# Retention and a mixture of experts on one core: the first two batches in another token layout, with 64x64 score tiles and states summed afresh

## The chip, the cores and the metric

One core of a Trainium2 chip. The metric is the device time of one launch in microseconds (us), all runs below being in the undisturbed state ("fast") by the granted clock and by agreement with the other runs of the same kernel. A profile is one execution taken by the hardware profiler; its span is about 1.7 us shorter than the launch's time.

Two words for the tensor engine (TensorE, PE): I call it **full rate** where a 512-column matmul follows the last after 0.216 us and **half rate** where it takes 0.43 us. The prediction says "fast state" and "slow state" for the same thing. Read the rate from the spacing of the matmuls: the clock column of the views reads 1.00 for the start, though 128 columns take 0.106 us through most of it, as against 0.057 at full rate.

## The reference

```python
# q, k, v: [8 batches, 8 heads, 576 tokens, 64], float32
scores = q @ k.transpose(0, 1, 3, 2) / sqrt(64)
Dmat   = where(i >= j, gamma[h] ** (i - j), 0)           # decay, one gamma for each head
x      = ((scores * Dmat) @ v)                           # retention
x      = x.transpose(0, 2, 1, 3).reshape(4608, 512)      # tokens x (heads * 64)
p      = domain_probs / domain_probs.sum(-1)
out    = sum over 4 experts of  p[:, e] * (relu(x @ w1[e]) @ w2[e])   # 512 -> 1024 -> 512
```

## The kernel before

Expert work is done in nine tiles of 512 tokens. Each tile has 48 groups, 12 for each expert (8 of the first matrix, then 4 of the second), 256 matmuls of 128x512 in all. While tile `nt` runs, the retention of batch `nt + 1` is put between its groups by a plan (`at(group, function)`). Batch 0 must be done before the first tile. Decay is split into factors on k (`gk`) and on the result (`gq`), so a chunk of 128 tokens needs its own masked scores and the state, the sum of `k^T v` over all earlier chunks. Two heads share a "pair". An eviction copies a result of TensorE out of PSUM, the memory that it writes to; a mask is VectorE's copy of the scores with those above the diagonal set to zero.

```python
    def load(b, gate=None):                      # 24 transfers of 128 KB in 256 B packets
        t = {n: raw.tile([128, NCH, H, D], FP32, tag=n, name=f"raw_{n}") for n, _ in SRC}
        for p in range(NP):
            for n, src in SRC:
                for h in (2 * p, 2 * p + 1):
                    i = nc.sync.dma_start(out=t[n][:, :, h, :],
                                          in_=src[b, h, 0:SM, :].rearrange("(c p) d -> p c d", p=C))
        # ... cut: gate: the first transfer waits for another DMA

        def kv(self, n, pairs):                  # the chain: add chunk n to the state in PSUM, copy it out
            # ... cut: matmuls into self.kvp
            for j in (0, 64):
                nc.scalar.activation(sbd[n][j:j + 64, a:z, j:j + 64],
                                     self.kvp[j:j + 64, a:z, j:j + 64], Copy)

    for p in allp:                               # batch 0, one pair after the other
        casts0(p)
        if p > 0:
            a0.O([p - 1])                        # outputs of the last pair
        a0.T(p)                                  # transposes of q and k
        a0.kv(0, [p])
        a0.S([p])                                # scores, masks
        for n in range(1, NCH):
            a0.kv(n, [p])
    # ... cut: weights of experts 1 to 3
    load(1, a0.w20)                              # batch 1, released when w2 of expert 0 has landed

        if nt == 0:                              # the plan of tile 0
            # ... cut: the remainder (tokens 512 to 575) of batch 0
            for p, g in zip(allp, (22, 31, 40, 44)):
                at(g - 4, *[lambda p=p, n=n: state["a1"].cast(n, p, nc.gpsimd) for n in "kqv"])
                at(g, lambda p=p: state["a1"].T(p), lambda p=p: state["a1"].kv(0, [p]))
                at(g + 1, lambda p=p: state["a1"].kv(1, [p]), lambda p=p: state["a1"].S([p]))
                at(g + 2, lambda p=p: state["a1"].kv(2, [p]))
                at(g + 3, lambda p=p: state["a1"].kv(3, [p]), lambda p=p: state["a1"].O([p]))
            at(46, lambda: state["a1"].cast_rem(nc.gpsimd))
            at(47, lambda: state["a1"].Trem(), lambda: state["a1"].Srem(), lambda: state["a1"].Orem())
            at(47, lambda: load(2), lambda: load_rem(2))
```

Later batches are transposed by DMA instead of TensorE and run inside full tiles.

## Time and profile before

| | before |
|---|---|
| time, median | 591.28 us (587.73 to 591.89, 3 runs) |
| span of the profiled run | 590.0 us |
| TensorE busy | 94% of the span |
| start, until the first expert matmul | 28.3 us |
| tile 0, tile 1, tile 2 | 75.5, 70.1, 60.3 us |

"Busy" counts time with an instruction in flight; for pipelined matmuls that is not peak use. To see where a tile loses time, compare it with a tile in the steady state: tile 2 and those after it are full. The prediction below shows the view of these stretches, the waits and the two holes.

### The profile page before, as it was taken

The numbers are of one execution on the slowest core, as the hardware profiler recorded it, in microseconds if no ns is written. First come the engines' busy times: TensorE is split into PE (matmuls) and PEld (weight loads), VectorE is DVE, ScalarE is ACT, GpSimd is POOL, SyncE is SP. The second block draws the span as 40 slices with busy tenths as digits, with TensorE's granted clock in tenths as the row PEclk, the third lists the DMA queues.
The fourth block names the chain that finished last, engine by engine and source line by source line (L and its number), as shares of the span: only waits on it lengthen the run. The fifth ranks groups of instructions, "written<-read, shape, count | busy, mean of one in ns | idle before, by whom it ended". The sixth has DMA issues, their size and how long they took to land.

```text
span 590.0 us, 8114 instructions
## 1 busy us (share of the span) xinstructions
PE 554.6 (94%) x3223; PEld 262.9 (45%) x3284; DVE 162.7 (28%) x268; ACT 232.3 (39%) x446; POOL 89.5 (15%) x131
## 2 busy tenths in 40 slices
PE   3698798779999999999999999999999999999997
PEld 2344354334444444444444444444444444444443
DVE  5512136004420442034303430343124311220222
ACT  5443343443236323632354335433453344335332
POOL 3510320342400411031203130223000000000000
PEclk9999799979999999999999999999999999999999
DMA  8999922948225901490149104820400010010001
GB/s 200 187 202 201 214 55 75 211 103 193 54 80 90 223 1 59 96 224 17 53 100 214 28 37 111 188 59 19 124 11 1 4 69 1 0 49 23 1 0 71
DMA packets 155157, 53.82 MB, mean 91 GB/s; under 512 B 144332, under 2 KB 148428, under 8 KB 155120
## 3 DMA queue, kind: packets, MB, share of 16 engines
q1 hardware_dynamic: 148848, 44.92, 31.9%
q0 software_dynamic: 6272, 8.39, 8.1%
q8 instruction: 25, 0.41, 0.3%
q14 instruction: 12, 0.10, 0.1%
HBM read 45.16 MB, written 9.44 MB: 93 GB/s over the span
## 4 chain that ended last, share of the span: by engine, by line
PE 84%; DMA 8%; SPq 5%; issue 1%; POOL 1%; ACT 0%; DVE 0%; POOLq 0%
PE po L305 40%; PE ph L298 38%; SPq L80 5%; DMA raw_v<-in_v_dram 4%; DMA wt_276<-in_moe_w_dram 3%; PE o L265 1%; PE kvp L195 1%; PE o L270 1%; POOL vm L182 1%; DMA raw_q<-in_q_dram 0%; POOL qm L182 0%; DVE acc L312 0%; PE orem L281 0%; PE pt L208 0%; PE orem L285 0%
## 5 line engine op out<-in xcount | busy, mean ns | idle before, releaser
L300 ACT ACTIVATE hT<-ph 128x512 bf16<-128x512 f32 x288 | 171.9, 597 | 263.8 <-PE ph L298 260.2
L305 PEld LDWEIGHTS <-hT 128*128 128x128 bf16 x1152 | 112.2, 99 | 139.2 <-issue 9.0
L312 DVE SCALAR_TENSOR_TENSOR acc<-po,probs,acc 128x512 f32<-128x512 f32 x108 | 81.1, 751 | 324.3 <-PE po L305 282.8
L298 PE MATMUL ph<-xT,wt_383 128*128 128x512 bf16 x281 | 66.3, 383 | 0.4
L305 PE MATMUL po<-wt_276,hT 128*128 128x512 bf16 x285 | 66.0, 386 | 0.3 <-issue 0.2
L305 PE MATMUL po<-wt_381,hT 128*128 128x512 bf16 x279 | 65.2, 386 | 1.1 <-issue 0.9
L298 PE MATMUL ph<-xT,wt_387 128*128 128x512 bf16 x279 | 65.4, 380 | 0.4
L298 PE MATMUL ph<-xT,wt_379 128*128 128x512 bf16 x279 | 65.3, 379 | 0.5
L298 PE MATMUL ph<-xT,wt_274 128*128 128x512 bf16 x280 | 64.0, 383 | 0.6 <-issue 0.2
L305 PE MATMUL po<-wt_385,hT 128*128 128x512 bf16 x279 | 63.6, 379 | 0.5
L305 PE MATMUL po<-wt_389,hT 128*128 128x512 bf16 x281 | 63.5, 379 | 0.4
L177 POOL TENSOR_TENSOR km<-raw_k,gk 128x512 bf16<-128x512 f32 x28 | 29.3, 1047 | 203.9 <-DMA raw_k<-in_k_dram 110.0
L298 PEld LDWEIGHTS <-wt_274 128*128 128x128 bf16 x288 | 28.4, 99 | 34.2 <-issue 1.6
L298 PEld LDWEIGHTS <-wt_383 128*128 128x128 bf16 x288 | 27.4, 98 | 31.8 <-issue 1.0
L298 PEld LDWEIGHTS <-wt_379 128*128 128x128 bf16 x288 | 27.3, 98 | 29.3
L298 PEld LDWEIGHTS <-wt_387 128*128 128x128 bf16 x288 | 26.9, 98 | 29.5
L310 ACT ACTIVATE acc<-po,probs 128x512 f32<-128x512 f32 x36 | 24.7, 687 | 38.1 <-PE po L305 37.1
L195 PE MATMUL kvp<-vm,km 128*128 128x128 bf16 x128 | 18.1, 230 | 16.0 <-POOL vm L182 11.4
L182 POOL CAST vm<-raw_v 128x512 bf16<-128x512 f32 x32 | 18.6, 613 | 80.2 <-PE o L265 60.8
L274 DVE TENSOR_TENSOR xT<-o,gq 128x512 bf16<-128x512 f32 x32 | 21.0, 688 | 19.4 <-PE o L270 18.8
L195 PEld LDWEIGHTS <-km 128*128 128x128 bf16 x128 | 10.7, 101 | 18.2 <-issue 11.5
L182 POOL CAST qm<-raw_q 128x512 bf16<-128x512 f32 x28 | 16.1, 612 | 10.4 <-DMA raw_q<-in_q_dram 10.4
(231 smaller groups left out, 249.4 us busy)
## 6 DMA issues: line engine op xcount, KB each, us to landing
out_dram<-acc SPq DMA_DIRECT2D x36, 256.0 KB, 2.0
raw_k<-in_k_dram SPq DMA_DIRECT2D x64, 128.0 KB, 2.9
raw_q<-in_q_dram SPq DMA_DIRECT2D x64, 128.0 KB, 2.8
raw_v<-in_v_dram SPq DMA_DIRECT2D x64, 128.0 KB, 2.8
wt_274<-in_moe_w_dram POOLq DMA_DIRECT2D x1, 1024.0 KB, 9.7
raw_kr<-in_k_dram SPq DMA_DIRECT2D x8, 128.0 KB, 3.5
wt_276<-in_moe_w_dram POOLq DMA_DIRECT2D x1, 1024.0 KB, 15.9
raw_qr<-in_q_dram SPq DMA_DIRECT2D x8, 128.0 KB, 3.2
```

Source lines behind the costliest of these rows:

```text
L80: i = nc.sync.dma_start(out=t[n][:, :, h, :], in_=src[b, h, 0:SM, :].rearrange("(c p) d -> p c d", p=C))
L177: self.gate[n, p] = eng.tensor_tensor(o, i, gk[:, 0:NCH, h].unsqueeze(3).to_broadcast([128, NCH, 2, D]), op=MULT)
L182: self.gate[n, p] = eng.tensor_copy(o, i)
L195: nc.tensor.matmul(self.kvp[:, p, :], lhsT=flat(self.m["k"][:, n, h, :]), rhs=flat(self.m["v"][:, n, h, :]), start=(n == 0 and i == 0), st ...
L265: nc.tensor.matmul(o[64 * j:64 * j + 64, c * C:(c + 1) * C], lhsT=self.m["v"][:, c, 2 * p + j, :], rhs=self.sT[p][:, j, c, :], start=(c == ...
L270: nc.tensor.matmul(o[:, c * C:(c + 1) * C], lhsT=sbd[c - 1][:, p, :], rhs=self.qkT[:, 0, p, c * C:(c + 1) * C], start=False, stop=(c == NC ...
L274: nc.vector.tensor_tensor(xT[:, p, b * S:b * S + SM], o, gq[:, p, 0:SM], op=MULT)
L298: nc.tensor.matmul(ph, lhsT=w1_sb[e][:, dc, fc * 128:(fc + 1) * 128], rhs=xT[:, dc, n0:n0 + NT], start=(dc == 0), stop=(dc == NDC - 1))
L300: nc.scalar.activation(hT[:, fc, :], ph, Relu)
L305: nc.tensor.matmul(po, lhsT=hT[:, fc, ns * 128:(ns + 1) * 128], rhs=w2_sb[e][:, fc, :], start=(fc == 0), stop=(fc == NFC - 1))
L310: nc.scalar.activation(acc[ns], po, Copy, scale=pe)
L312: nc.vector.scalar_tensor_tensor(acc[ns], po, pe, acc[ns], op0=MULT, op1=ADD)
```

## The change

The intent: load batches 0 and 1 with two neighbouring tokens on one partition, which makes packets of 512 B, in units of four heads by 256 tokens (`hf` is the half, `u` the four heads); tile the scores 64x64, so that four small matmuls run at once (no score less is computed: 16 matmuls of 64x64x128 for a unit, where a pair had 8 of 64x128x128, and the masks keep their size); sum each state from scratch, so that no state waits for the eviction of the one before; let the first three groups of tile 0 start on 256 tokens (`lead`). Batch 2 is loaded earlier, into half buffers. Not shown: k of batch 0 is cast by GpSimd instead of VectorE, w1 of expert 0 comes in two transfers, and later batches are loaded and cast by chunk. Cut to its core:

```diff
+                    if b < 2:
+                        h = slice(4 * u, 4 * u + 4)
+                        i = nc.sync.dma_start(
+                            out=pairs_of(t[n, hf])[:, h],
+                            in_=src[b, h, 256 * hf:256 * hf + 256, :].rearrange("h (p j) d -> p h (j d)", j=2))
+                    else:            # by chunk, 256 B packets as before
...
+        def kv(self, hf, u):
+            for s in range(2):
+                rows = [(slice(0, 128), x) for x in range(2 * hf)]
+                rows += [(slice(0, 64 + 64 * s), 2 * hf + j) for j in range(2)]
+                ...                  # 8 matmuls in the first half, 16 in the second
...
-    for p in allp:
-        casts0(p)
-        if p > 0:
-            a0.O([p - 1])
-        a0.T(p)
-        a0.kv(0, [p])
-        a0.S([p])
-        for n in range(1, NCH):
-            a0.kv(n, [p])
+    for x, (hf, u) in enumerate(UNITS):
+        ...                          # casts; two exponentials for gq in units 0 and 1
+        a0.T(hf, u, nc.scalar)
+        a0.kv(hf, u)
+        a0.S(hf, u)
+        a0.O(hf, u)
...
-            for p, g in zip(allp, (22, 31, 40, 44)):
+            for x, g in zip(UNITS, (17, 24, 32, 39)):
+                ...                  # casts at g-3, T at g, kv at g+1, S at g+2, O at g+5
-            at(47, lambda: load(2), lambda: load_rem(2))
+            at(37, lambda: load(2), lambda: load_rem(2))
+            ...                      # remainder of batch 1: groups 42, 43, 45, 46 instead of 46, 47
-        for g, _ in enumerate(moe(nt)):
+        for g, _ in enumerate(moe(nt, lead=3 if nt == 0 else 0)):
```

## The prediction

> **What bounds the kernel now.** I read the page first (TensorE is busy 94% of the span, the chain that ended last is 84% TensorE), then cut the span at the tile boundaries that the timeline shows: the first expert matmul starts at 28.3 us, tile 0 (512 tokens) ends at 103.8, tile 1 at 173.9, tile 2 at 234.2. The windows view of these four stretches (start:end, length, busy us and count of each engine, granted clock, DMA share, GB/s):
>
> ```profile
> 0.00:28.30 28.30, 14.02 (x125) 8.58 (x127) 15.09 (x41) 14.03 (x42) 12.09 (x24) 1.00 1.00 193
> 28.30:103.80 75.50, 68.88 (x430) 32.78 (x437) 23.91 (x41) 28.05 (x68) 12.36 (x17) 0.95 0.79 151
> 103.80:173.90 70.10, 62.48 (x366) 29.26 (x374) 17.22 (x27) 24.51 (x44) 21.61 (x30) 0.95 0.53 124
> 173.90:234.20 60.30, 59.93 (x363) 28.49 (x368) 17.55 (x27) 24.41 (x44) 10.86 (x15) 1.00 0.43 97
> ```
>
> Tile 2 is the steady state: 60.3 us, TensorE full. 256 expert matmuls at 0.216 us (eight take 1.73 us in the chain) are 55.3 us; the other 5 us are the attention of the next batch. The tiles after it repeat, the last ones without attention. So everything outside the first 174 us is at the matmul bound and the change, which touches batches 0 and 1 (and how later batches are loaded and cast, beside full tiles), can only move the first three rows: 28.3 us of start, a tile of 75.5 and a tile of 70.1.
>
> What they lose is in TensorE's waits (line, releaser: total us, times, longest):
>
> ```profile
> PE kvp L195 <- POOL vm L182: 11.4, 5, 6.2
> PE pt L208 <- ACT qm L180: 7.1, 4, 6.5
> PE kvp L195 <- ACT sbd_162 L200: 2.3, 5, 0.5
> ```
>
> and the timeline shows the two large holes, in tile 0 and in tile 1, and the slow matmuls after each:
>
> ```profile
> 61.27 0.61 POOL L182 CAST vm<-raw_v 128x512 bf16<-128x512 f32 x1 [8.59 <-DMA raw_v<-in_v_dram]
> 61.94 0.26 PE L195 MATMUL kvp<-vm,km 128*128 128x128 bf16 x1 [4.40 <-POOL vm L182]
> 62.85 2.76 PE L305 MATMUL po<-wt_381,hT 128*128 128x512 bf16 x6 [0.22 <-issue]
> ...
> 120.54 0.26 PE L195 MATMUL kvp<-vm,km 128*128 128x128 bf16 x1 [6.15 <-POOL vm L182]
> ```
>
> First hole: batch 1's v is late by DMA, TensorE waits 4.4 us, then 12 expert matmuls run at 0.43 us instead of 0.216 (2.5 us) and some attention slowly too: about 7.4 us. Second hole: the load of batch 2 is issued only at 101.8 us, after tile 0's output stores, its casts end at 120 us, and TensorE sits for over 6 us and restarts slowly. Tile 1 is 70.1 - 60.3 = 9.8 us too long. The start is a dependency chain, not a load: pair 1 of batch 0 begins at 6.50, pair 2 at 11.94, pairs 3 and 4 at 17.38 and 22.83, a period of 5.44 us, while a pair's 786 KB are issued in 3.3 us. One period:
>
> ```profile
> 6.50 0.61 PE L208 MATMUL pt<-ident,qm 128*128 128x128 bf16 x4 [6.50 <-ACT qm L180]
> 7.57 0.69 DVE L209 COPY qkT<-pt 128x1024 bf16<-128x1024 bf16 x1 [2.56 <-PE pt L208]
> ...
> 9.03 0.69 DVE L237 TENSOR_TENSOR sT<-s_197,tri 128x512 bf16<-128x512 f32 x1 [0.77 <-PE s_198 L230]
> ...
> 9.64 0.68 DVE L237 TENSOR_TENSOR sT<-s_198,tri 128x512 bf16<-128x512 f32 x1
> ...
> 10.48 0.27 PE L195 MATMUL kvp<-vm,km 128*128 128x128 bf16 x1 [0.53 <-ACT sbd_162 L200]
> ...
> 10.67 0.64 PE L265 MATMUL o<-sT,vm 128*64 128x128 bf16 x8
> ```
>
> The masks end at 10.32; the serial chain of states (matmul, ScalarE eviction, matmul) ends at 10.5. The chain that the change removes therefore lies almost wholly beside the masks: without it the outputs could start only some 0.3 us earlier.
>
> **The Trainium skill.** (1) "TensorE: Matmul & The Clock Gate", Part 1: the array runs at 1.2 GHz until about 3.4 us of sustained activity and falls back after idle of that order. The trace agrees: 0.43 us per 512 columns after the holes, 0.216 otherwise; the whole start runs slow (128 columns every 0.106 us at 6.5 to 27 us, 0.057 later). (2) "DMA: Bandwidth & Descriptors", Queues, rings and completion order: an engine takes turns between queues by packet. The trace agrees: between the release of batch 1's load at 30.8 and 61.3 us five weight matrices landed (3 x 512 + 2 x 1024 rows = 3584 packets) and some 3072 packets of 256 B of batch 1, nearly one to one. (3) Same page, Specifications: line rate wants at least 512 B per transfer. The trace has 256 B packets at about 235 GB/s alone; no run yet shows 512 B. (4) "TensorEngine Tiling (Array Packing)", Key Properties: a change of tiling mode drains the array. The trace shows it between 64-row scores and 128-row states as about 0.14 us extra when slow, about 0.1 when fast.
>
> **Part by part.**
>
> Loads of batches 0 and 1. Two tokens per partition make 512 B packets, 12 transfers of 256 KB instead of 24. Taking turns by packet, batch 1 gets twice the bytes per weight packet: one w1 (512 packets) lets 262 KB through, one w2 524 KB, so a w1 and a w2 together carry one unit's 786 KB. I estimate batch 0 landed at 13 us, w1 of expert 0 at 19.5, its w2 at 25 (before: 30.7), which releases batch 1. From the weights' spacing before (about 5.8 us a w1, 6.6 a w2, some 10% longer now), units 0 to 3 of batch 1 land at about 40, 53, 67 and 70 us. They are wanted at groups 17, 24, 32 and 39, by my sum about 51, 63, 72 and 85 us. The first hole closes: 7.4 us gained.
>
> Load of batch 2. It is placed at group 37 instead of 47, ahead of the output stores, and its buffers are halves that come free with the casts. It can run from about 72 to 87 us. Tile 1 then finds its data and should take the steady 60.3: 9.8 us gained. This is the largest and safest term.
>
> More TensorE work in tile 0. From the timeline one pair of batch 1 in the fast state displaces 0.51 (8 transposes and a state) + 0.49 + 0.06 + 0.68 = 1.74 us, four pairs 7.0. A unit after: 8 transposes 0.45; 8 or 16 state matmuls at 0.057 (each state summed from scratch) with 2 or 4 changes between 64 and 128 rows, 0.65 or 1.3; 16 scores of 64x64 (twice as many, four at a time; weight loads of 64 columns take 0.022 each) 0.65; 16 outputs and 2 to 4 state products 0.8. Sum 2.5 or 3.25, four units 11.5: 4.5 us lost. The remainder of batch 1 was a serial 2.6 us at group 47 (101.2 to 103.8); spread over groups 43 to 46 it is about 0.8: 1.8 gained. Tile 0: 75.5 - 7.4 + 4.5 - 1.8 = 70.8.
>
> The start. Scheduled unit by unit without interleaving: transposes, states, scores, outputs. In the slow state: transposes 0.85; states 1.15 or 2.3 (16 x 0.106 and four drains); scores 0.7 and 0.3 to the end; two masks 1.3 as above; outputs 0.7, drain 0.2, state products 0.2 or 0.4. Periods about 5.7 and 7.1 us, four units 25.6. First transpose: the query cast no longer stands behind four exponentials (3.1 us on ScalarE), so about 4.7 us in place of 6.5, allowing for two of them before the eviction. Experts start at 4.7 + 25.6 = 30.3, 2.0 us later than now. Should TensorE go fast, as it is denser now, transposes, states and outputs halve, periods fall to some 4.9 and 5.5 and the start ends at 25.6, 2.7 us earlier. The lead of three half-width groups only hides the last eviction, under 1 us.
>
> Sum. Slow start: -2.0 + (75.5 - 70.8 = 4.7) + 9.8 = 12.5 us less. Fast start: 2.7 + 4.7 + 9.8 = 17.2 less. I weigh them 60 to 40: 14.4 us off 591.3, so 576.9; I say 576.5.
>
> **Rivals.** (a) The start is the load, not the chain: then 512 B packets and more of them per turn would bring the experts forward by 5 us or more, total near 570. For: TensorE's longest single wait, 6.5 us, is for the first data. Against: data is issued every 3.3 us but used every 5.44. (b) The hole in tile 0 moves rather than closes: unit 2 is wanted at 72 and lands at 67 plus 2.3 us of casts (1.05 + 0.61 + 0.61), a margin of 3 us that a faster start eats. If it is missed, 2 to 4 us of wait and a slow restart: total 581 to 583. (c) 64x64 scores run no better than two at a time and the weight loads bind, 0.05 us each slow: another 3 us in start and tile 0, 580. (d) Later tiles slow because casts go by chunk: against it, GpSimd is busy 11 of 60 us there and TensorE has no waits.
>
> **Range and chances.** The two safe terms, 9.8 and 7.4, less 2.7 of surer extra work, leave 14.5; the start moves this by -3 to +6, rivals b and c by another -4. That gives 569 to 583. A 2% gain needs 579.4, which the slow start (578.8) only just meets; I put 0.75 on faster, 0.24 on same, 0.01 on slower.
>
> **What would show it.** Right: no wait for v over 1 us after the start; tile 1 at 60 to 61 us; batch 2's load issued before 80 us; tile 0 at 69 to 72; expert matmuls from 26 to 31 us; masks (0.68 each) still between scores and outputs in each unit. Wrong: experts beginning before 25 us (the chain was load or the clock); a hole in tile 0 at a unit's transposes or states; tile 1 longer than 62 us.

## The result and the profile after

The changed kernel takes **576.12 us** (574.53 to 577.0, 4 runs), against 591.59 us of the kernel before in the same comparison (4 runs, the three above among them). The ratio is 0.9747 with a 95% interval from 0.9698 to 0.9796. Ratios here are the mean time of one kernel's fast runs over that of the other's of the same rounds, so not quite the ratio of the medians quoted. The span of the profiled run is 572.8 us.

The windows view of the changed kernel, cut as before at the first expert matmul and the tile boundaries (columns as in the prediction: start:end, length, then PE, PEld, DVE, ACT and POOL busy, clock, DMA share, GB/s):

```profile
0.00:27.10 27.10, 16.92 (x220) 11.89 (x221) 11.40 (x36) 12.64 (x26) 19.35 (x35) 1.00 1.09 214
27.10:96.20 69.10, 67.94 (x542) 34.25 (x549) 25.74 (x54) 24.77 (x44) 18.89 (x26) 1.00 1.04 204
96.20:156.60 60.40, 60.03 (x363) 28.61 (x369) 17.54 (x27) 24.41 (x44) 13.80 (x20) 1.00 0.47 94
156.60:216.90 60.30, 59.84 (x363) 28.52 (x369) 17.54 (x27) 24.41 (x44) 10.68 (x15) 1.00 0.47 97
```

The reader is to see three differences: the start 28.3 to 27.1, tile 0 75.5 to 69.1, tile 1 70.1 to 60.4 us. They sum to 1.2 + 6.4 + 9.7 = 17.3, and the spans differ by 590.0 - 572.8 = 17.2. (The medians differ by 15.5: the profiled run of the changed kernel was its fastest.) Tile 2 is 60.3 us in both. (The 28.3 is probably some 0.4 us too late: three later kernels with the same start (experiments 2 to 4) show a first expert matmul at 27.87 that this trace lacks. What the start gains is then 0.8 us and tile 0 6.8.)

TensorE's waits in the changed kernel, complete but for one of 0.3 us (line, releaser: total us, times, longest):

```profile
PE pt L330 <- ACT qm L320: 5.3, 1, 5.3
PE o L386 <- DVE sT L374: 4.4, 8, 0.9
PE kvp L352 <- POOL vm L322: 0.5, 1, 0.5
```

The 11.4 us for v have become 0.5. The chain's waits on ScalarE evictions are gone: 4.4 us in nine waits, of which the view in the prediction shows 2.3 for one of the states. In their place stand 4.4 us in eight waits of the outputs for the masks. One unit of the start, in the timeline:

```profile
5.28 0.61 PE L330 MATMUL pt<-ident,qm 128*128 128x128 bf16 x4 [5.28 <-ACT qm L320]
...
6.36 1.12 PE L352 MATMUL kvp<-vm,km 64*128 64x128 bf16 x8
...
8.55 0.69 DVE L374 TENSOR_TENSOR sT<-s_194,tri_134 128x512 bf16<-128x512 f32 x1 [0.81 <-PE s_195 L369]
9.15 0.68 DVE L374 TENSOR_TENSOR sT<-s_195,tri_134 128x512 bf16<-128x512 f32 x1
...
9.89 0.63 PE L386 MATMUL o<-sT,vm 64*64 64x128 bf16 x14 [0.28 <-DVE sT L374]
...
10.64 0.63 PE L330 MATMUL pt<-ident,qm 128*128 128x128 bf16 x4
```

The outputs now wait for both masks (0.28 us for the second after 0.86 for the first); before, TensorE waited for the chain there and the outputs began 0.35 us after the second mask's end. They still stand behind the masks, and the next unit cannot begin ahead of them: its period is 10.64 - 5.28 = 5.36 us, the others 5.05, 6.14 and 5.28, against 5.44 for each pair before. Only in the last unit, at about 24.5 us, do matmuls reach full rate.

The loads, from the DMA queue's and GpSimd's timelines:

```profile
46.76 0.62 POOL L322 CAST vm<-raw_v 128x512 bf16<-128x512 f32 x1 [4.21 <-DMA raw_v<-in_v_dram]
...
61.05 0.62 POOL L322 CAST vm<-raw_v 128x512 bf16<-128x512 f32 x1 [4.17 <-DMA raw_v<-in_v_dram]
```

```profile
69.77 1.01 SPq L90 DMA_DIRECT2D raw_k<-in_k_dram  x1
...
90.52 7.00 SPq L440 DMA_DIRECT2D out_dram<-acc  x4
```

The v of batch 1's first two units lands at 46.7 and 61.0 us. At 61 us the kernel before had only the first pair of four, a quarter of the batch; now half of it is there. Batch 2 is asked for at 69.8 us, well ahead of the output stores.

What the prediction could not yet show, the rate of 512 B packets, stands in the windows view from 5 to 10 us, when batch 0 alone is loading. First the kernel before, then the changed kernel:

```profile
5.00:10.00 5.00, 2.24 (x19) 1.46 (x20) 1.67 (x4) 2.33 (x8) 0.70 (x2) 1.00 1.04 235
5.00:10.00 5.00, 3.23 (x40) 2.26 (x44) 1.71 (x3) 4.72 (x10) 3.04 (x5) 1.00 1.12 297
```

The last column rises from 235 to 297 GB/s; with batch 0 back in 256 B packets (experiment 6) it is 230.

### The profile page after: what moved, and what is told of

The parts are those of the page before. It is cut to its first block, busy times and chain, and to the rows that moved or that the text cites. A ratio compares the mean times of both kernels' runs of the same rounds, so it can differ in the third digit from the quotient of the medians.

```text
span 572.8 us, 8376 instructions
## 1 busy us (share of the span) xinstructions
PE 554.1 (97%) x3426; PEld 267.1 (47%) x3488; DVE 161.2 (28%) x277; ACT 227.5 (40%) x406; POOL 94.9 (17%) x140
## 4 chain that ended last, share of the span: by engine, by line
PE 88%; DMA 7%; SPq 3%; issue 1%; POOL 1%; DVE 0%
PE po L431 41%; PE ph L409 40%; DMA raw_v<-in_v_dram 4%; SPq L85 3%; DMA wt_469<-in_moe_w_dram 2%; PE o L285 1%; PE kvp L223 1%; DMA raw_k<-in_k_dram 1%; PE o L290 1%; PE kvp L352 1%; PE orem L301 0%; POOL wt_389 L116 0%; PE orem L305 0%; POOL vm L322 0%; PE o L386 0%
## 5 line engine op out<-in xcount | busy, mean ns | idle before, releaser
L409 PE MATMUL ph<-xT,wt_471 128*128 128x512 bf16 x286 | 66.0, 379 | 0.1
L409 PE MATMUL ph<-xT,wt_475 128*128 128x512 bf16 x274 | 64.8, 379 | 0.5
L409 PE MATMUL ph<-xT,wt_479 128*128 128x512 bf16 x272 | 64.5, 379 | 0.5
L409 PE MATMUL ph<-xT,wt_389 128*128 128x512 bf16 (+1 forms) x291 | 63.4, 370 | 0.5
L208 POOL TENSOR_TENSOR km<-raw_k,gk 128x512 bf16<-128x512 f32 x24 | 25.1, 1044 | 121.6 <-DMA raw_q<-in_q_dram 48.3
L210 POOL CAST vm<-raw_v 128x512 bf16<-128x512 f32 x24 | 14.8, 616 | 130.0 <-PE o L285 126.0
L294 DVE TENSOR_TENSOR xT<-o,gq 128x512 bf16<-128x512 f32 x24 | 15.5, 686 | 11.1 <-PE o L290 10.6
L228 ACT ACTIVATE sbd<-kvp 64x256 bf16<-64x256 f32 x48 | 17.8, 372 | 0.3
L210 POOL CAST qm<-raw_q 128x512 bf16<-128x512 f32 x24 | 14.7, 611 | 0.4 <-POOL km L208 0.3
L318 POOL TENSOR_TENSOR km<-raw_k,gk 128x512 bf16<-128x512 f32 x8 | 8.3, 1042 | 22.1 <-DMA raw_k<-in_k_dram 22.1
```

Source lines behind the costliest of these rows:

```text
L208: eng.tensor_tensor(o, i, gk[:, c, :].unsqueeze(2).to_broadcast([128, H, D]), op=MULT)
L210: eng.tensor_copy(o, i)
L228: nc.scalar.activation(sbd[j:j + 64, n, a:z, j:j + 64], self.kvp[j:j + 64, a:z, j:j + 64], Copy)
L294: nc.vector.tensor_tensor(xT[:, p, b * S:b * S + SM], o, gq[:, p, 0:SM], op=MULT)
L318: eng.tensor_tensor(o, i, g.unsqueeze(3).to_broadcast([128, 2, 4, D]), op=MULT)
L409: nc.tensor.matmul(ph[:, ts], lhsT=w1_sb[e][:, dc, fc * 128:(fc + 1) * 128], rhs=xT[:, dc, n0 + ts.start:n0 + ts.stop], start=(dc == 0), s ...
```

## The experiments

Twelve kernels ran, all with the right result. Each is compared with the kernel before on the same chip; I give the median and that ratio. The kernel before took 590.55, 589.82 and 591.12 us in the three sets of rounds.

**1. `a_load2_late`: batch 2's load back behind the stores.**

```diff
-            at(37, lambda: load(2), lambda: load_rem(2))
+            at(47, lambda: load(2), lambda: load_rem(2))
```

> The changed kernel with the load of batch 2 back at group 47, behind tile 0's output stores. My theory: when that load is issued decides tile 1. It would be issued at about 98 us instead of 70; chunks now land in the order in which they are used, so the state matmuls of chunk 0 still find data, but chunk 3 (landing about 113 us) and the transposes behind it come late: tile 1 grows from 60.5 by 3 to 6 us, total 579 to 583. Rival 1: the early issue is all of it and the whole hole of before returns, 9 to 10 us, total 586. Rival 2: half buffers and chunk order alone close the hole, total within 1 us of 576.

Measured: 584.25 us, ratio 0.9892 (0.9865 to 0.9919). It loses 8.1 us, more than I expected and nearly the hole of before. Its waits:

```profile
PE s L250 <- DMA qkT<-km: 4.7, 2, 2.4
...
PE kvp L223 <- POOL vm L210: 1.0, 1, 1.0
```

Loading by chunk does what I thought for the states (1.0 us of wait instead of 6), but the scores then wait twice for the DMA transposes. These are issued on the load's own queue, the first at 115.2 us behind the load's last transfer, and run one behind another. The time at which this load is issued is worth 8 us of the changed kernel's 15.

**2. `b_load2_early`: the kernel before, with that load moved and nothing else.**

```diff
-            at(47, lambda: load(2), lambda: load_rem(2))
+            at(41, lambda: load(2))
+            at(47, lambda: load_rem(2))
```

> The kernel before, with nothing but the load of batch 2 moved from group 47 to group 41 (just behind the last casts that read its buffers, ahead of the output stores). My theory: it would be issued at about 78 us, land by 93, and tile 1 falls from 70.1 to about 61; total 581 to 583, so some 60% of the whole change's gain without any change of layout. Rival: the order of casts in that kernel (all k, all q, all v) still makes the states wait for v; tile 1 stays above 65 and the total above 586.

Measured: 582.25 us, ratio 0.9862 (0.9842 to 0.9883). As expected: 8.3 us for one moved line, with no state waiting in tile 1, which takes 60.3 us (103.45 to 163.74). The rival, that the order of casts would keep the hole, falls. The hole in tile 0 stays:

```profile
PE kvp L195 <- POOL vm L182: 4.3, 1, 4.3
```

**3. `b_placed`: the same, with batch 1's pairs at later groups.**

```diff
-            for p, g in zip(allp, (22, 31, 40, 44)):
+            for p, g in zip(allp, (27, 33, 38, 43)):
```

> As the last one, and the four pairs of batch 1 moved from groups 22, 31, 40, 44 to 27, 33, 38, 43, to where their data has landed. My theory: the hole in tile 0 is a matter of place too; v of pair 0 lands at 61.2 us and group 27 comes at about 62, so tile 0 loses its 7.4 us and the total is 573 to 576, as good as the changed kernel or better, with 256 B packets, one token per partition and the serial chain. Rival: without larger packets the data cannot feed tile 0 and a hole of 3 us or more stays; total above 578.

Measured: 577.09 us, ratio 0.9763 (0.9736 to 0.9790). No wait for v is left in tile 0, with 256 B packets: the v of the first pair is cast at 60.8 us, ahead of its new place. I had hoped for 573 to 576. The last stretch of the tile shows what is missing:

```profile
94.91 0.28 PE L215 MATMUL ptr<-ident,krb 64*128 64x64 bf16 x4
96.03 0.31 PE L251 MATMUL sr<-qkT 64*64 64x64 bf16 x8 [0.84 <-DVE qkT L216]
96.84 0.61 PE L281 MATMUL orem<-sTr,vrb 64*64 64x64 bf16 x8 [0.50 <-DVE sTr L255]
97.39 0.29 PE L285 MATMUL orem<-qkT,sbd 128*128 128x64 bf16 x4
97.51 8.76 PE L298 MATMUL ph<-xT,wt 128*128 128x512 bf16 x32
```

The remainder's three steps wait for each other at group 47, and behind it 32 expert matmuls take 8.76 us, some at half rate. Behind the same waits in experiment 2 they took 7.07, all at full rate; why the two differ stays open.

**4. `b_placed_rem`: the same, with the remainder spread.** (The remainder of batch 2 is also loaded at group 43 instead of 47.)

```diff
+            at(42, lambda: state["a1"].cast_rem(nc.gpsimd))
+            at(43, lambda: state["a1"].Trem())
+            at(45, lambda: state["a1"].Srem())
+            at(47, lambda: state["a1"].Orem())
```

> The kernel before with places alone changed: load of batch 2 at group 41, pairs of batch 1 at groups 27, 33, 38, 43, and now the remainder of batch 1 spread over groups 43 to 47 instead of one serial stretch at 47 that took 2.7 us. My theory: 1.5 to 2 us less than with the first two places alone (577.1): 575 to 576, level with the changed kernel or better, with none of its new layout, tiling or states. Rival: the remainder's waits only move; no gain, 577.

Measured: 573.36 us, ratio 0.9723 (0.9697 to 0.9748). This is 2.5 to 3.7 us less than without the spread (by the ratios 0.4%, by the medians 0.6%; the two sets of rounds differ). The kernel before, with work moved in the plan of tile 0 and nothing else, is level with the changed kernel: the intervals of 0.9723 and 0.9747 overlap, so I don't call it faster. In the traces the old kernel's start, tile 0 and tile 1 now take 27.9, 67.9 and 60.3 us, the changed kernel's 27.1, 69.1 and 60.4.

**5. `a_b1_256`: 256 B packets for batch 1 only.** The same bytes go to the same places, in two transfers for each one before, one for each token of a partition.

```diff
+                        if b == 1:
+                            for j in range(2):
+                                i = nc.sync.dma_start(out=o.rearrange("p h (j d) -> p h j d", j=2)[:, :, j, :],
+                                                      in_=s.rearrange("h (p j) d -> p h j d", j=2)[:, :, j, :])
```

> The changed kernel with batch 1 alone loaded in 256 B packets (each transfer in two, one for each token of a partition). My theory: TensorE's place for unit 0 (group 17, about 49.5 us) needs the doubled bytes per turn; with 256 B the v of unit 0 lands at about 60 us as it did before, TensorE waits about 10 us at the states of unit 0 and restarts slowly for 2 to 3 us; total 586 to 590. Rival: packet size does not matter and the earlier release is what helped; total within 2 us of 576.

Measured: 585.10 us, ratio 0.9911 (0.9891 to 0.9930). The predicted wait is there:

```profile
58.51 0.62 POOL L329 CAST vm<-raw_v 128x512 bf16<-128x512 f32 x1 [8.49 <-DMA raw_v<-in_v_dram]
...
59.17 1.12 PE L359 MATMUL kvp<-vm,km 64*128 64x128 bf16 x8 [7.62 <-POOL vm L329]
```

The v of the first unit lands at 58.5 us instead of 46.7, and it costs 9 us: TensorE waits 1.6 us for q and 7.6 for v. The total is just under the range that I gave. So at the changed kernel's early places the 512 B packets are necessary. Experiment 3 says what they are necessary for: for those places, which are not themselves needed. (The changed kernel with small packets and later places was not run.)

**6. `a_b0_256`: 256 B packets for batch 0 only.** The same edit with `b == 0`.

> The changed kernel with batch 0 alone loaded in 256 B packets (24 issues instead of 12). My theory: the start is a chain and not the load; first transposes at about 5.9 us instead of 5.3, experts begin less than 1.2 us later (28.3 at most). What it does cost is behind that: the weights are issued 2 us later, so batch 1 is released 2 us later and the wait for the v of its second unit grows to about 2.5 us; total 578 to 579. Rival (my rival a): the load bounds the start; experts begin 3 us or more later, after 30 us.

Measured: 576.68 us, ratio 0.9778 (0.9751 to 0.9805), beside 0.9747. The first transposes begin at 6.28 us instead of 5.28 and the experts at 28.34 instead of 27.11. The start moves by the delay of its first data, and no more of the load shows in it, so the rival falls. The cost behind it, 1 us in waits for v (1.4 instead of 0.5), is smaller than I expected, and so is the total; its interval overlaps that of the changed kernel.

**7. `a_chain`: the serial chain of states put back.** One running sum for each pair stays in PSUM; 4 matmuls and an eviction come before the scores, 4 and an eviction after them.

```diff
-        a0.kv(hf, u)
-        a0.S(hf, u)
+        a0.kv(hf, u, 0)          # rows 0:64 added to self.kvp, state copied out
+        a0.S(hf, u)
+        a0.kv(hf, u, 1)          # rows 64:128 added
```

> The changed kernel with the serial chain of states put back: one running sum per pair in PSUM, a step of 4 matmuls (64 rows) and its eviction before the scores, the second step after them. My theory: the chain lay beside the masks and its removal bought nothing; with it back the two units of the second half lose 8 of 16 state matmuls each before their scores. Experts begin at about 25.7 us instead of 27.1 and tile 0 displaces some 0.5 us less; but the v of batch 1's second unit still lands at about 61 us, so its wait grows from 0.5 to about 2 us and eats most of it: total 575 to 576. Rival (the change's own intent): the chain costs the start 2 us or more; experts begin after 29 us, total above 578.

Measured: 574.69 us, ratio 0.9737 (0.9706 to 0.9769), level with the changed kernel's 0.9747 and not above it. Experts begin at 26.33 us; unit periods are 5.35, 5.07, 5.26 and 5.26. The waits on the masks are halved because the second step of the chain runs in them:

```profile
PE s L367 <- DVE qkT L340: 2.3, 4, 0.7
PE o L384 <- DVE sT L372: 2.2, 8, 0.3
```

The wait for v that I expected to grow did not: TensorE reached full rate later here (the first 20 expert matmuls took 4.39 us, 2.35 in the changed kernel), which used up the time saved. What the run settles is the direction: removing the chain bought nothing.

**8. `h_pipe_late`: chain, outputs one unit behind, later places.** The outputs of unit `x-1` come after the transposes and the first states of unit `x`, so the masks run beside matmuls.

```diff
+        a0.T(hf, u, nc.scalar)
+        a0.kv(hf, u, 0)
+        if x < 3:
+            casts0(x + 1)
+        if x < 2:
+            load_gq((2 * x, 2 * x + 1))
+        if x > 0:
+            a0.O(*UNITS[x - 1])
+        a0.S(hf, u)
+        a0.kv(hf, u, 1)
-            for x, g in zip(UNITS, (17, 24, 32, 39)):
+            for x, g in zip(UNITS, (20, 30, 35, 40)):
```

> Meant to beat both: the changed kernel with the serial chain back and, in the start, the outputs of a unit issued behind the transposes and first states of the next one, so that TensorE does not sit through the masks (4.4 us of waits in eight steps in the changed kernel); the units of batch 1 placed at groups 20, 30, 35, 40, where their data has landed. My theory: experts begin at 23 to 24.5 us, no wait over 0.5 us in tile 0, total 570 to 573. Rival: the load then bounds the start (a unit needs 3 us to land) and experts do not begin before 26 us, total 574 or more.

Measured: 571.33 us, ratio 0.9684 (0.9655 to 0.9714), which just overlaps the changed kernel's interval; only experiment 11 is clear of it. Experts begin at 23.44 us, and tile 0 has no wait for v. The rival, that the load would bound this, falls. The masks no longer separate scores and outputs:

```profile
17.83 0.60 PE L330 MATMUL pt<-ident,qm 128*128 128x128 bf16 x4
...
18.79 0.60 PE L350 MATMUL kvp<-vm,km 64*128 64x128 bf16 x4
19.33 0.64 PE L384 MATMUL o<-sT,vm 64*64 64x128 bf16 x16
```

**9. `a_pipe`: the same without the chain,** states summed from scratch as in the changed kernel.

> As h_pipe_late (outputs of a unit behind the next unit's transposes and states, batch 1 at groups 20, 30, 35, 40), but the states summed from scratch as in the changed kernel: it parts the gain of that run. My theory: the order of the outputs is most of it; experts begin at 24 to 25.5 us (23.4 with the chain, 27.1 in the changed kernel), total 571.5 to 574. Rival: the chain is what made the interleaving short; experts begin after 26 us.

Measured: 573.27 us (569.21 to 573.65), ratio 0.9691 (0.9654 to 0.9728). Experts begin at 25.16 us. Of the 3.7 us by which experiment 8 shortens the start, the order of the outputs gives 1.95 and the chain another 1.7, where it gave 0.8 without that order (experiment 7). A likely reason, not tested apart: a unit of the second half has 16 state matmuls in a row (2.37 us) without the chain, two steps of 4 (0.6 us each) with it. In the total the two cannot be told apart.

**10. `a_warm`: ten matmuls of 128x512 ahead of everything,** their result unread, in the changed kernel.

```diff
+    wz = const.tile([128, 512], BF16)
+    nc.vector.memset(wz, 1.0)
+    pw = ps_mm.tile([128, NT], FP32, tag="mm", name="pw")
+    for _ in range(10):
+        nc.tensor.matmul(pw, lhsT=wz[:, 0:128], rhs=wz, start=True, stop=True)
```

> The changed kernel with ten idle matmuls of 128x512 ahead of everything, from about 1 to 5 us, whose result nobody reads, so that TensorE meets the first data in its fast state. It tests the two cases of my prediction. My theory: with the transposes, states and outputs at full clock the four units take 4.4 to 4.7 us each instead of 5.05 to 6.14, and experts begin at 23.5 to 24.5 us instead of 27.1; but the v of batch 1's second unit still lands at about 61 us, so its wait grows from 0.5 us to 3 to 4 us and takes it all back: total 575 to 577. Rival 1: the array falls back to the slow state in the gaps of the first unit, experts begin after 26.5. Rival 2: tile 0 has slack and the total falls by the same 3 us, to 573.

Measured: 575.58 us, ratio 0.9745 (0.9714 to 0.9775): no gain, but not for my reason. The timeline:

```profile
1.52 4.45 PE L131 MATMUL pw<-wz 128*128 128x512 bf16 x10 [1.52 <-DVE wz L128]
...
7.12 0.71 PE L358 MATMUL kvp<-vm,km 64*128 64x128 bf16 x8 [0.41 <-POOL vm L328]
...
11.50 1.15 PE L358 MATMUL kvp<-vm,km 64*128 64x128 bf16 x8
```

Eight state matmuls take 0.71 us in the first unit (full rate) and 1.15 in the second (half rate). The full rate was lost again within one unit, though no wait of TensorE there exceeded 0.9 us. Here the clock column shows it too: 0.98 from 6 to 10 us, 0.50 from 10 to 15. Experts begin at 27.84. My theory falls and the first rival holds.

**11. `h_warm`: experiment 8 with the ten matmuls, and the first two exponentials ahead of the first query cast.**

```diff
+    load_gq((0, 1))              # and pos_i, which they read, made earlier
     casts0(0)
...
-        if x < 2:
-            load_gq((2 * x, 2 * x + 1))
+        if x == 1:
+            load_gq((2, 3))
```

> The best candidate: h_pipe_late with the ten idle matmuls at the beginning, and the first two exponentials for the query decay before the first query cast, while ScalarE waits for data. My theory: units then take about 3 us of TensorE each, the load of a unit takes as long, experts begin at 20 to 21.5 us, the weights of expert 0 (second matrix at about 29 us) just arrive; total 567 to 570. Rival: the weights are late and TensorE waits for them; total as h_pipe_late, 571.

Measured: **568.96 us** (568.72 to 570.38, 5 runs), ratio 0.9638 (0.9614 to 0.9662). It beats the changed kernel (0.9747, interval from 0.9698) and is the best; its lead over experiment 8 is not clear of the intervals. Experts begin at 22.29 us, not at 20 to 21.5 as I expected: the states of the second unit already run at half rate again:

```profile
7.48 0.38 PE L356 MATMUL kvp<-vm,km 64*128 64x128 bf16 x4 [0.70 <-POOL vm L328]
...
10.15 0.58 PE L356 MATMUL kvp<-vm,km 64*128 64x128 bf16 x4 [0.29 <-POOL vm L328]
```

Which of its two edits helped was not tested apart; after experiment 10 I would look at the exponentials first.

**12. `a_lead0`: no lead.**

```diff
-        for g, _ in enumerate(moe(nt, lead=3 if nt == 0 else 0)):
+        for g, _ in enumerate(moe(nt, lead=0)):
```

> The changed kernel without the lead (the first three groups of tile 0 in two halves of 256 tokens). My theory: it hides only the last eviction of batch 0's attention; without it the third matmul of the first group waits 0.5 us for that eviction, nothing else changes: total within 0.8 us of 576. Rival: the lead lets the experts start while the second half is still in work and is worth 2 us or more.

Measured: 575.55 us (2 runs), ratio 0.9745. One wait of 0.3 us for the last eviction appears, and the time is the same.

## Why the prediction was right, point by point

The time, 576.5 predicted and 576.12 measured, came out closer than its parts.

**The bound.** Right: tile 2 is 60.3 us before and after, and all of the gain lies in the first three stretches.

**Load of batch 2.** Right: tile 1 is 60.4 us. Experiments 1 and 2 show the same 8 us from both sides. I had put 9.8 on it, and in experiment 2's trace the moved line alone gives all of that (tile 1 70.1 to 60.3, spans 590.0 and 580.0). The medians of its rounds differ by 8.3; the kernel before ran from 589.2 to 591.7 us in them.

**First hole.** Right that it closes, and that turns by packet are the reason (experiment 5). In size it was nearer 6.0 than 7.4: that is how much shorter tile 0 became when only the pairs were moved (75.6 us in experiment 2, 69.6 in 3). Wrong in size were the landings. I had units 0 and 1 of batch 1 at 40 and 53 us; they landed at 46.7 and 61.0. I had rounded 3072 packets against 3584 to "nearly one to one". Between the release at 28.4 and 61.0 us it was again about 3072 of 512 B against three w1 and just over two w2, 0.85 to one. The release came 3.4 us later than I had it, as w2 of expert 0 landed at 28.3 instead of 25. A margin of 10 us for unit 1 was really none: TensorE waited 0.5 us there. My rival (b) named unit 2 for this, which had time; unit 1 did not.

**More work in tile 0.** Right in sign, too large in size. A unit displaces 0.44 + 0.66 + 0.45 + 0.50 = 2.05 us in the first half and 0.44 + 1.31 + 0.45 + 0.60 = 2.80 in the second, 9.7 for four instead of my 11.5. What I had too dear were scores and outputs: I took the loading of weights as their limit. The 64x64 tiles really run four at a time, and rival (c) falls: the start times of 16 scores go up in four steps of 0.056 us at full rate, 0.106 at half rate. Tile 0 took 69.1 us, where I had 70.8.

**The start.** Half right. The chain of states did lie beside the masks (experiment 7), the masks did stay between scores and outputs, and the load was not the bound (experiment 6). Sizes failed: "Periods about 5.7 and 7.1 us" at half rate were 5.36, 5.05 and 6.14. Part of that is my own sum: the parts that I list add to 5.4 and 6.75. Of the rest, the scores' issue took 0.33 us for my 0.7, and the outputs with the drain behind them 0.57 for my 0.9. And of my two cases neither happened: TensorE stayed at half rate for three units and reached full rate in the fourth. Experts began at 27.1 us, between my 30.3 and 25.6. My weighing of 60 to 40 gave 28.4. That it was near is luck of the weights, not knowledge of the clock; experiment 10 shows that I did not know what keeps it. Under (1) I took an idle stretch of some 3.4 us to be what ends the full rate; there it ended with no wait over 0.9 us.

**Where the gain came from.** The title's three means account for less of the 15 us than their bulk suggests. Moving lines in the plan of the old kernel gives 8.3 us (experiment 2), 13.5 (3) and 16.5 (4). The packets pay for the earlier places only; states from scratch and the lead pay nothing that shows. The tiles' own worth was not measured by itself, but little can come of them here: the scores of a unit take four steps of 0.106 us at half rate, and so did those of a pair before, two at a time with twice the columns of weights each. What won was a start in which outputs follow one unit behind, with the chain back and batch 1 at later places (experiments 8 and 11). The old kernel, with the places of experiment 4, was not tried with that order.

## What to carry to other kernels

Before changing layouts or instructions, look for work that is issued too late or placed where its data has not landed: two holes of TensorE stood here, and moving a few lines closed both and gained 13.5 us (experiment 3). A serial chain is worth removing only where it is the last thing waited for; here it ran beside the masks, and reordering so that something else runs beside the masks was what shortened the start (by 1.95 us in experiment 9). When two DMA queues share the engines, count packets, not bytes, to see when each will be served, and don't round the share.

## What the Trainium skill lacked or had wrong

- "TensorE: Matmul & The Clock Gate", Part 1, speaks of busy and idle windows, and of short idles that can make the rate go up and down, but gives no measure of how dense the work must be. In experiment 10 the array had run ten dense matmuls for 4.45 us, was then never waiting longer than 0.9 us, and ran at half rate again from about 10 us, 4 us after the last of them; in the kernel before it stayed at half rate through the whole start, with 14 of 28 us busy.
- "DMA: Bandwidth & Descriptors", Queues, rings and completion order, does not say how the turns come out in bytes when the runs of two queues differ in length. Here some 0.85 contiguous run, of 256 B before and of 512 B after, landed for each weight row of 1 or 2 KB, so that doubling the run about doubled the bytes per row (experiment 5: v at 46.7 against 58.5 us). How many of them make one turn, no experiment here shows.
- "TensorEngine Tiling (Array Packing)" gives four 64x64 tiles as independent and was borne out: four matmuls in each step of 0.056 us. That the drain between modes costs about 0.1 us at full rate it does not say.
